# The nine scatters of the output: with and without a wait for the one before

## The chip, the core and the metric

The kernel runs on one core of a Trainium2 chip. The core has five engines, each with a list of instructions of its own: TensorE (PE, matmuls; PEld is its weight load), VectorE (DVE), ScalarE (ACT), GpSimd (POOL) and SyncE (SP). They wait for each other by semaphores. Transfers between the chip's memory and the core's own memory run on 16 DMA engines; they are issued by SyncE (queue q1) and, where an index decides which rows are written or read, by GpSimd (queue q0). The metric is the time of one execution in microseconds of device time, the median of several.

## The reference

Three parts follow each other: causal attention in a window of 128 positions with a linear bias (batch 2, 8 heads, 576 positions, 64 columns), a mixture of 8 experts in which each token goes to the expert with the largest logit, and a second mixture in which each token goes to every expert. There are N = 1152 tokens of D = 512 columns, and the hidden width F is 1024. The last part ends in the output that this change is about:

```python
for e in range(E):
    h = np.maximum(x @ w1[e], 0.0)
    ye = h @ w2[e]
    out += P[:, e:e + 1] * ye
return out.astype(np.float32)
```

`P` are weights of tokens and experts, normalized eight times over experts and over tokens.

## The kernel before, in words

After the first mixture the tokens lie sorted by expert, not in the order of the input. The table `tok_i` (128 rows by 9) holds for each place of the sorted order the token that stands there; it is a permutation of the 1152 tokens, together with the places of its nine columns. It is made on the chip with scatters of line 1021 and read back once. The first mixture takes its tokens with indexed gathers (`load_x`, line 243). Both go through GpSimd's queue and are over early.

The second mixture works on the sorted tokens. Its sums are held in nine tiles `acc[0]` to `acc[8]` of 128 tokens by 512 columns. Expert 0 is done first. The other seven experts are done in 14 passes (`passes`, two for each expert, each with half of the hidden units). In a pass, `group` makes hidden units for a part of the tokens (its matmuls are line 1360, its other work lines 1351 to 1373 on ScalarE and VectorE), and `layer2` multiplies them with the second weights. For each tile `layer2` runs 12 matmuls (line 1391) into one bank of PSUM, and VectorE then adds the bank, weighted by `Pm`, to `acc[s]` (line 1393). Matrix products are made in three parts from values that are split in a high and a low part; GpSimd makes some of the low parts (lines 1247 and 1254).

In the last pass alone, each `acc[s]` is final after line 1393 and goes out at once: GpSimd issues a scatter (line 1395) that writes the 128 rows of the tile to the rows of `out` that `tok_i[:, s]` names. That is 256 KB a scatter, nine in all. The nine sums of the last pass stand one right behind the other on VectorE, in the order of the tiles of two groups (four tiles and then five), and the nine scatters are the last work on GpSimd.

The order on each engine is the order in which the code is written (`in_order` ties each instruction to the one before it on its engine). The waits between engines are put in by the tile framework, by what each instruction reads and writes. It takes a scatter with an index as a write to all of `out`, so that a scatter has to wait for the landing of the scatter before it. A transfer that GpSimd issues takes one of eight semaphore lanes in turn, and it waits until the earlier transfer on its own lane has landed. When the last instruction is done, the engines wait for all lanes and meet in a closing barrier; those instructions have line 1448.

Of the kernel before, what the change touches and what calls it, by code (L numbers as in the profile page):

```python
# [89 lines left out]
def fused_kernel(ctx, tc, q, k, v, wg1, w1, w2, wg2, u1, u2, out, capacity):  # L90
    nc = tc.nc
# [1165 lines left out]
    def run(steps, count=99):  # L1257
        for _ in range(count):
            if next(steps, 0) == 0:
                break  # L1260
# [81 lines left out]
    def bank():  # L1342
        return ring.tile([P, DM], F32, tag="pr", name="pr")
# [39 lines left out]
    def layer2(n, g, steps):  # L1383
        e, r = passes[n]
        for s in TILES[g]:
            run(steps, 2)
            ops = bank()
            m = 0
            for k in range(2 * QP):
                for a, b in ((hT[0], w2p[0]), (hT[0], w2p[1]), (hT[1], w2p[0])):  # L1390
                    nc.tensor.matmul(ops, a[:, k, s * P:(s + 1) * P], b[:, k, :], start=(m == 0), stop=(m == 6 * QP - 1))  # L1391
                    m += 1
            nc.vector.scalar_tensor_tensor(out=acc[s], in0=ops, scalar=Pm[:, s, e:e + 1], in1=acc[s], op0=ALU.mult, op1=ALU.add)  # L1393
            if n == len(passes) - 1:
                nc.gpsimd.indirect_dma_start(  # L1395
                    out=out[:, :], out_offset=IndirectOffsetOnAxis(ap=tok_i[:, s:s + 1], axis=0),
                    in_=acc[s], in_offset=None)
        run(steps)

    last_of.update({k: None for k in last_of})  # L1400
    n0 = len(nc.cur_bb.bb.instructions)
    load_2(0)
    for n in range(len(passes) + 1):
        more = n < len(passes)
        if n == 0:
            run(parts_y(0))
            load_1(1)
        if more:
            for q in range(QP):
                group(q, 0)  # L1410
        if n:
            layer2(n - 1, 1, iter(()))
        if more:
            psteps = parts_2(n)
            weight_sums(n + 1)
            for q in range(QP):
                run(psteps, QP)
                group(q, 1)
            load_2(n + 1)

            def both():
                for st_ in (parts_x(n + 1), parts_y(n + 1)):
                    for _ in st_:
                        yield 1
                load_1(n + 2)

            layer2(n, 0, both() if n + 1 < len(passes) else iter(()))
        in_order(n0)
        n0 = len(nc.cur_bb.bb.instructions)
# [22 lines left out]
```

## Time and profile before

| what | value |
|---|---|
| median of 3 runs | 1060.69 us |
| lowest and highest of the runs | 1059.94 and 1061.14 us |
| time of the profiled execution | 1050.62 us |
| its span, from the first to the last instruction | 1048.4 us |
| mean granted TensorE clock | 0.994 |
| TensorE busy | 1019.7 us, 97% |
| GpSimd busy | 320.1 us, 31% |

The span is what the views of the profile divide. The time of the profiled execution is 2.2 us more than its span, and the median of the runs is 10.07 us above the profiled execution. Times in the views are microseconds from the start of the span. A queue's own instructions, like waits for semaphores, carry a q behind the engine's name and count as no busy time.

### The profile page before, as it was taken

The page shows a single profiled execution, that of the slowest core. Times are in us where ns is not written, and L with a number is a line of the kernel's source. Part 1 is how long each engine was busy: PE and PEld are TensorE (multiplying, and loading weights), DVE is VectorE, ACT ScalarE, POOL GpSimd, SP SyncE. Part 2 cuts the span into 40 slices and gives each one's busy share as a digit, 9 for nine tenths or more (in the row PEclk, how much of TensorE's full clock was granted, in tenths as well). Part 3 has the DMA queues.
Part 4 walks back from the last instruction along what each step waited for, and adds up shares of the span by engine and source line. Part 5 has one row for each costly group of instructions (what it writes and reads, how often), then busy time and mean ns, then how long its engine had stood idle before and what let it go on. Part 6 is the DMA issues. An engine that isn't in the chain of part 4 may idle for free. (4 is left out here: it accounts for less than half of the span.)

```text
span 1048.4 us, 16893 instructions
## 1 busy us (share of the span) xinstructions
PE 1019.7 (97%) x6420; PEld 929.7 (89%) x6420; DVE 674.8 (64%) x1636; ACT 387.1 (37%) x838; POOL 320.1 (31%) x305
## 2 busy tenths in 40 slices
PE   8999999999999999999999999999999999999994
PEld 6888999998889998989899999989899999989893
DVE  7987778777784347575765757574665757575551
ACT  7643577777321313232232323232232323233220
POOL 7433244431200123341323224231333324132122
PEclk9999999999999999999999999999999999999998
DMA  9921599885200102021111202021111202021001
GB/s 244 217 54 52 168 252 228 239 249 197 79 1 1 63 19 81 1 81 41 41 41 41 81 1 81 1 81 42 41 41 41 81 1 81 9 72 41 1 21 70
DMA packets 74104, 83.24 MB, mean 79 GB/s; under 512 B 31585, under 2 KB 45921, under 8 KB 74018
## 3 DMA queue, kind: packets, MB, share of 16 engines
q1 hardware_dynamic: 71906, 76.59, 25.3%
q0 software_dynamic: 2112, 5.52, 1.7%
q8 instruction: 52, 0.85, 0.3%
q14 instruction: 34, 0.28, 0.1%
HBM read 77.37 MB, written 4.73 MB: 78 GB/s over the span
## 5 line engine op out<-in xcount | busy, mean ns | idle before, releaser
L1391 PE MATMUL pr<-w_whi,hT 128*128 128x512 f32 x1008 | 315.8, 390 | 0.3 <-DVE hT L1352 0.3
L1391 PEld LDWEIGHTS pr<-w_whi,hT 128*128 128x128 f32 x1008 | 189.3, 188 | 39.4 <-DVE hT L1352 0.5
L1391 PE MATMUL pr<-w_wlo,hT 128*128 128x512 f32 x504 | 196.5, 390 | 0.0
L1254 POOL TENSOR_TENSOR w_wlo<-r,w_whi 128x512 fp32r<-128x512 f32 x56 | 71.3, 1294 | 291.0 <-ACT w_whi L1253 181.1
L1393 DVE SCALAR_TENSOR_TENSOR acc<-pr,Pm,acc 128x512 f32<-128x512 f32 x126 | 91.2, 744 | 89.8 <-PE pr L1391 89.7
L1351 ACT ACTIVATE hT<-pr 128x256 fp32r<-128x256 f32 (+1 forms) x168 | 69.0, 411 | 175.6 <-DVE pr L1368 175.6
L1352 DVE SCALAR_TENSOR_TENSOR hT<-pr,hT 128x256 fp32r<-128x256 f32 (+1 forms) x168 | 77.0, 458 | 80.1 <-ACT hT L1351 80.1
L1360 PE MATMUL pr<-y_hi,wy 128*128 128x320 f32 (+1 forms) x560 | 122.7, 297 | 0.0
L1391 PEld LDWEIGHTS pr<-w_wlo,hT 128*128 128x128 f32 x504 | 94.7, 188 | 19.5 <-POOL w_wlo L1254 0.5
L1360 PEld LDWEIGHTS pr<-y_hi,wy 128*128 128x128 f32 x560 | 93.8, 188 | 0.3 <-DVE hT L1352 0.3
L1247 POOL TENSOR_TENSOR wy<-r,wy 128x512 fp32r<-128x512 f32 x28 | 40.0, 1428 | 174.2 <-ACT wy L1246 174.2
L191 DVE TENSOR_TENSOR wlo<-w,whi 128x1024 fp32r<-128x1024 f32 x66 | 81.7, 1241 | 3.1 <-issue 3.1
L1360 PE MATMUL pr<-y_lo,wy 128*128 128x256 f32 (+1 forms) x280 | 83.3, 297 | 0.0
L179 ACT CAST whi<-w 128x1024 fp32r<-128x1024 f32 x66 | 69.1, 1050 | 22.4 <-DMA w<-in_moe_w_dram 18.0
L748 PE MATMUL pb<-xt,whi 128*128 128x384 f32 x256 | 74.3, 362 | 2.5 <-issue 1.9
L748 PE MATMUL pb<-h,whi 128*128 128x384 f32 x256 | 75.5, 362 | 1.2 <-DVE t L768 1.2
L1253 ACT CAST w_whi<-r 128x512 fp32r<-128x512 f32 x56 | 33.1, 619 | 94.9 <-PE pr L1391 94.0
L1351 ACT ACTIVATE hT<-h 128x256 fp32r<-128x256 f32 (+1 forms) x56 | 24.9, 445 | 115.4 <-DVE h L1368 115.4
L1360 PE MATMUL pr<-y_hi,wx_wlo 128*128 128x256 f32 (+1 forms) x224 | 64.6, 289 | 0.0
L1360 PE MATMUL pr<-y_hi,wx_whi 128*128 128x256 f32 (+1 forms) x224 | 64.4, 288 | 0.0
L1360 PE MATMUL pr<-y_lo,wx_whi 128*128 128x256 f32 (+1 forms) x224 | 64.4, 288 | 0.0
L1231 POOL TENSOR_TENSOR sums<-r 128x512 f32<-128x512 f32 x28 | 37.1, 1327 | 80.3 <-DMA r<-in_moe_w_dram 45.9
(358 smaller groups left out, 2255.7 us busy)
## 6 DMA issues: line engine op xcount, KB each, us to landing
w<-in_moe_w_dram SPq DMA_DIRECT2D x36, 1024.0 KB, 7.9
r<-in_moe_w_dram SPq DMA_DIRECT2D x56, 512.0 KB, 3.9
kb<-in_k_dram SPq DMA_DIRECT2D x8, 256.0 KB, 4.4
qb<-in_q_dram SPq DMA_DIRECT2D x8, 256.0 KB, 4.5
vb<-in_v_dram SPq DMA_DIRECT2D x8, 256.0 KB, 5.4
xg_d<-xg SPq DMA_DIRECT2D x8, 256.0 KB, 2.6
kb<-in_k_dram SPq DMA_DIRECT2D x2, 128.0 KB, 4.6
qb<-in_q_dram SPq DMA_DIRECT2D x2, 128.0 KB, 4.9
```

The costliest lines, as they stand in the source:

```text
L179: nc.scalar.copy(his[i][:, sl, :], raws[i][:, sl, :])
L191: nc.vector.tensor_tensor(out=los[i][:, sl, :], in0=raws[i][:, sl, :], in1=his[i][:, sl, :].bitcast(F32), op=ALU.subtract)
L748: nc.tensor.matmul(ps[:, 0:2 * W], whi, x.rearrange("p r w -> p (r w)"), start=(m == 0), stop=(m == K - 1))
L1231: nc.gpsimd.tensor_tensor(out=o[:, dst], in0=x, in1=y, op=op_)
L1247: nc.gpsimd.tensor_tensor(out=wy[1][:, i], in0=x, in1=wy[0][:, i].bitcast(F32), op=ALU.subtract)
L1253: nc.scalar.copy(w2p[0][:, k], x)
L1254: nc.gpsimd.tensor_tensor(out=w2p[1][:, k], in0=x, in1=w2p[0][:, k].bitcast(F32), op=ALU.subtract)
L1351: nc.scalar.activation(hi, src, AF.Relu)
L1352: nc.vector.scalar_tensor_tensor(out=lo, in0=src, scalar=0.0, in1=hi.bitcast(F32), op0=ALU.max, op1=ALU.subtract)
L1360: nc.tensor.matmul(ps, a[:, i, c, f], b, start=(c == 0 and m == 0), stop=(c == 1 and m == 2))
L1391: nc.tensor.matmul(ops, a[:, k, s * P:(s + 1) * P], b[:, k, :], start=(m == 0), stop=(m == 6 * QP - 1))
L1393: nc.vector.scalar_tensor_tensor(out=acc[s], in0=ops, scalar=Pm[:, s, e:e + 1], in1=acc[s], op0=ALU.mult, op1=ALU.add)
```

## The change

Each scatter is remembered in a list, and each new one is declared to have no dependency on those remembered, so that the framework puts in no wait between them. The matrix `tok_i` names each row of `out` once, so no two of the scatters write the same row.

```diff
             if n == len(passes) - 1:
-                nc.gpsimd.indirect_dma_start(
+                st_op = nc.gpsimd.indirect_dma_start(
                     out=out[:, :], out_offset=IndirectOffsetOnAxis(ap=tok_i[:, s:s + 1], axis=0),
                     in_=acc[s], in_offset=None)
+
+                for before in stores:
+                    tc.declare_no_dep(st_op.ins, before, reason="rows of different tokens")
+                stores.append(st_op.ins)
         run(steps)
 
+    stores = []
     last_of.update({k: None for k in last_of})
```

The end of GpSimd's list in the kernel before, with what each instruction waits for (`DMASW0` to `DMASW7` are the eight lanes, `DVE` is VectorE, here the sum in `acc`):

```order
L1395 DMA out_dram<-acc,tok_i 1152x512 [waits DMASW3_49,DMASW2_49,DVE_49]
L1395 DMA out_dram<-acc,tok_i 1152x512 [waits DMASW4_49,DMASW3_49,DVE_49]
L1395 DMA out_dram<-acc,tok_i 1152x512 [waits DMASW5_49,DMASW4_49,DVE_49]
L1395 DMA out_dram<-acc,tok_i 1152x512 [waits DMASW6_49,DMASW5_49,DVE_49]
L1395 DMA out_dram<-acc,tok_i 1152x512 [waits DMASW7_49,DMASW6_49,DVE_49]
L1395 DMA out_dram<-acc,tok_i 1152x512 [waits DMASW7_49,DMASW0_49,DVE_49]
L1395 DMA out_dram<-acc,tok_i 1152x512 [waits DMASW1_49,DMASW0_49,DVE_49]
L1395 DMA out_dram<-acc,tok_i 1152x512 [waits DMASW2_49,DMASW1_49,DVE_49]
L1395 DMA out_dram<-acc,tok_i 1152x512 [waits DMASW2_49,DVE_49]
```

From the second on, each has the lane of the scatter before it among its waits; the first takes lane 3, the ninth lane 3 again. The same place in the changed kernel, on the same engine:

```order
L1395 DMA out_dram<-acc,tok_i 1152x512 [waits DMASW3_49,DMASW2_49,DVE_49]
L1395 DMA out_dram<-acc,tok_i 1152x512 [waits DMASW4_49,DVE_49]
L1395 DMA out_dram<-acc,tok_i 1152x512 [waits DMASW5_49,DVE_49]
L1395 DMA out_dram<-acc,tok_i 1152x512 [waits DMASW6_49,DVE_49]
L1395 DMA out_dram<-acc,tok_i 1152x512 [waits DMASW7_49,DVE_49]
L1395 DMA out_dram<-acc,tok_i 1152x512 [waits DMASW0_49,DVE_49]
L1395 DMA out_dram<-acc,tok_i 1152x512 [waits DMASW1_49,DVE_49]
L1395 DMA out_dram<-acc,tok_i 1152x512 [waits DMASW2_49,DVE_49]
L1395 DMA out_dram<-acc,tok_i 1152x512 [waits DMASW3_49,DVE_49]
```

Each has kept the wait for its own lane and for VectorE. The order of the instructions on the five engines is otherwise the same in both kernels; only line numbers behind the change are others (the closing line 1448 is 1453).

## Rows read from the trace of the kernel before

**Rows 1.** Head of the page: span, busy time of each engine
```profile
span 1048.4 us, 16893 instructions
PE 1019.7 (97%) x6420; PEld 929.7 (89%) x6420; DVE 674.8 (64%) x1636; ACT 387.1 (37%) x838; POOL 320.1 (31%) x305
```

**Rows 2.** Table by stretch: length, busy times, granted clock, DMA share, GB/s
```profile
108.00:130.00 22.00, 21.75 (x158) 21.55 (x159) 16.71 (x46) 12.99 (x21) 4.70 (x4) 1.00 0.57 181
155.00:182.00 27.00, 26.02 (x186) 25.62 (x185) 21.44 (x30) 19.96 (x33) 12.60 (x11) 1.00 0.94 248
1009.00:1033.00 24.00, 24.00 (x107) 19.73 (x106) 9.41 (x16) 1.50 (x4) 5.12 (x6) 1.00 0.14 55
1033.00:1048.40 15.40, 0.28 (x2) 0.00 (x0) 0.75 (x1) 0.00 (x0) 3.74 (x4) 0.68 0.17 68
```

**Rows 3.** Chain that ended last, its end: start, length, what
```profile
1037.33 2.54 issue
1039.87 2.71 DMA out_dram<-acc,tok_i
1042.58 0.02 issue
1042.60 0.02 POOLq L1395
...
1043.12 1.18 POOLq L1448
```

**Rows 4.** GpSimd in order of time: start, length, instruction, idle before, releaser
```profile
1015.28 1.20 POOL L1395 DMA_INDIRECT out_dram<-acc,tok_i  x1 [6.54 <-DVE acc L1393]
1019.00 0.96 POOL L1395 DMA_INDIRECT out_dram<-acc,tok_i  x1 [2.52 <-issue]
...
1025.92 0.96 POOL L1395 DMA_INDIRECT out_dram<-acc,tok_i  x1 [2.50 <-DVE acc L1393]
...
1032.91 0.96 POOL L1395 DMA_INDIRECT out_dram<-acc,tok_i  x1 [2.56 <-DMA out_dram<-acc,tok_i]
...
1043.35 0.96 POOL L1395 DMA_INDIRECT out_dram<-acc,tok_i  x1 [2.52 <-DMA out_dram<-acc,tok_i]
```

**Rows 5.** Line 1395, the scatters: ns shortest/median/longest; landing
```profile
L1395 POOL DMA_INDIRECT out_dram<-acc,tok_i x9: 958/958/1202, 1015.3 to 1043.3; - x9
...
DMA to landing us min/median/max: 2.7/2.7/2.9
```

**Rows 6.** VectorE in order of time: the first, third and ninth sum
```profile
1014.23 0.74 DVE L1393 SCALAR_TENSOR_TENSOR acc<-pr,Pm,acc 128x512 f32<-128x512 f32 x1
...
1017.00 0.75 DVE L1393 SCALAR_TENSOR_TENSOR acc<-pr,Pm,acc 128x512 f32<-128x512 f32 x1 [1.37 <-PE pr L1391]
...
1033.32 0.75 DVE L1393 SCALAR_TENSOR_TENSOR acc<-pr,Pm,acc 128x512 f32<-128x512 f32 x1 [1.97 <-PE pr L1391]
```

**Rows 7.** Lines 243 and 1021, indexed gathers and scatters earlier on
```profile
L243 POOL DMA_INDIRECT xw<-xg_d,slot_i x14: 916/1510/1939, 110.5 to 220.5; - x14
...
DMA to landing us min/median/max: 4.9/8.6/12.0
...
L1021 POOL DMA_INDIRECT tok_d<-tid_c,d_i x10: 950/1000/1899, 134.1 to 217.1; - x10
```

**Rows 8.** GpSimd from 110 to 113: two gathers, and their landings
```profile
110.52 0.94 POOL L243 DMA_INDIRECT xw<-xg_d,slot_i  x1 [11.54 <-DVE slot_i L654]
111.76 0.92 POOL L243 DMA_INDIRECT xw<-xg_d,slot_i  x1 [0.31 <-issue]
...
DMA to landing us min/median/max: 4.9/5.3/5.7
```

**Rows 9.** Line 1448 from 1034 on: the closing instructions of the queues
```profile
L1448 SPq EVENT_SEMAPHORE  x13: 17/28/20895, 1025.2 to 1048.4; - x13
...
L1448 POOLq DRAIN  x3: 52/115/4454, 1043.1 to 1048.1; - x3
```

**Rows 10.** DMA queues from 1036 to 1040, one scatter: packets, MB, share
```profile
DMA packets 80, 0.26 MB, mean 66 GB/s; under 512 B 16, under 2 KB 16, under 8 KB 80
...
q0 software_dynamic: 80, 0.26, 16.8%
```

## The prediction

> **What bounds the kernel now.** I read the top of the page first. TensorE is busy for 97% of the span [rows 1], so in nearly all of the 1048.4 us only work on TensorE could be saved. The table by stretch shows that this ends before the kernel does: up to 1033 TensorE is busy all the time at a granted clock of 1.00, and in the 15.4 us after 1033 it has 0.28 us of work, VectorE 0.75 us, ScalarE none [rows 2]. What fills these 15.4 us is the question, and the chain of waits answers it: a scatter of the output, a stretch of "issue", the next scatter, its landing 2.71 us after its start, a semaphore, and the closing instructions of line 1448 [rows 3]. Nothing else stands in that chain.
>
> Next I read GpSimd in order of time. The nine scatters of line 1395 start at 1015.28, 1019.00, and so on to 1043.35 [rows 4]. From the second to the ninth that is (1043.35 - 1019.00)/7 = 3.48 us each. Of it 0.96 us is GpSimd's own work and some 2.5 us idle time. The reader is to see that the idle time has the same length whatever the row names as its cause (issue, VectorE, or the scatter before). Its real cause is in the order with its waits: each scatter from the second on waits for the semaphore lane of the one before it, thus for its landing. A landing comes 2.7 us after the start [rows 5], and 3.48 - 2.71 = 0.77 us later the next one starts.
>
> VectorE, which makes the rows that are scattered, goes faster than that. Its nine sums of line 1393 come in steps of 2.72 us ((1033.32 - 1017.00)/6), the pace of 12 matmuls for a tile [rows 6]. So the scatters fall behind by 3.48 - 2.72 = 0.76 us with each tile, on top of the second one's delay. The last sum ends at 1033.32 + 0.75 = 1034.07, and its scatter starts at 1043.35, 9.28 us later. What is bound by the wait is thus the tail alone: a chain of nine transfers that ends last, beside a TensorE that has been done for ten microseconds.
>
> **The change, part by part.** It adds no instruction to any engine and moves none: TensorE, VectorE, ScalarE and SyncE keep their order, and the nine scatters keep theirs. Up to 1015 us nothing differs, and I count that part as 0.
>
> What it removes is the wait of the second to the ninth scatter for the lane of the one before. Two waits of each scatter stay: for VectorE's sum, and for the earlier use of its own lane. There are eight lanes. For the first eight scatters the lane was last used by the transfers of lines 243 and 1021, all issued by 220.5 us [rows 7]. The ninth has the lane of the first, which lands at 1015.28 + 2.9 = 1018.2 [rows 4, 5], 16 us before the ninth sum is there. So the lanes hold nothing up.
>
> What is late next is VectorE's sum. From the end of a sum to the start of a scatter that waits for nothing else there is one row: the first sum ends at 1014.23 + 0.74 = 1014.97 and its scatter starts at 1015.28, so 0.31 us [rows 4, 6]. GpSimd must also be free. Two indirect transfers with no wait between them start as soon as 0.30 us after the end of GpSimd's part of the one before: 110.52 + 0.94 to 111.76 [rows 8]. Scatter 2 then starts at about 1015.28 + 1.20 + 0.30 = 1016.8 and is out of GpSimd at 1017.7. Scatter 3 waits for its sum, which ends at 1017.75. From there on GpSimd needs 0.96 + 0.30 = 1.26 us in each 2.72 us, so it is never late again. Even the longest GpSimd part of any indirect transfer before, 1.94 us [rows 7], would give 2.24 us, still under 2.72.
>
> The ninth scatter: sum done 1034.07, plus 0.31, starts at 1034.38 in place of 1043.35. The saving is 1043.35 - 1034.38 = 8.97 us.
>
> What follows its start stays: 1048.4 - 1043.35 = 5.1 us to the end of the span. In it are 2.71 us to the landing (SyncE's long wait from 1025.2 of 20.9 us ends there, at 1046.1) and GpSimd's closing drain, 1043.1 + 4.45 = 1047.6 [rows 9], and then a barrier. Whether that drain hangs on the landing or on GpSimd's own end, it moves with the last scatter; TensorE's and VectorE's ends at 1034 are earlier than anything in it. So no part of the 5.1 us is saved.
>
> Does the landing stay at 2.71 us? Data of a scatter moves for some 0.7 us (16.8% of a 4 us stretch for its 80 packets [rows 10]). A scatter every 2.72 us and a landing after 2.71 us means that, but for the first two, hardly any two are in flight together, and no other traffic is left in that stretch: its DMA share of 0.14 before 1033 and 0.17 after is the scatters' own [rows 2]. I take 2.71.
>
> Bounds of what the trace does not show. The start after the sum: 0.31 us from the one row, or 0.77 us, what a scatter takes after a landing now; I take 0.31, since the ninth scatter, like the first, has had time to be decoded. GpSimd's part of the ninth: 0.96 us as in eight of nine [rows 5], or 1.94 as the longest [rows 7], which would put the landing 0.98 later; I take 0.96, as nothing runs beside it. The landing: 2.71, or 4.9 as the quickest of the gathers [rows 7], which is 2.2 more; I take 2.71, being the same transfer at the same load. Below these the saving can hardly go up: the scatter cannot start before 1034.07, which would add 0.31 us. Together the ends are a saving of 9.28 and one of 8.97 - 0.46 - 0.98 - 2.2 = 5.3 us.
>
> The sum: the profiled execution took 1050.62 us with a span of 1048.4; minus 8.97 gives a span of 1039.4 and 1041.65 us. The timed runs have a median of 1060.69, 10.07 us more than the profiled one. The trace has no row for that difference, so I keep it as it is: 1060.69 - 8.97 = 1051.7 us, 0.85% less.
>
> **The rivals.**
> 1. The queue takes one scatter at a time anyway. Then the scatters follow each other by 2.71 us in place of 3.48: the ninth lands at 1015.28 + 9 x 2.71 = 1039.67, against 1043.35 + 2.71 = 1046.06 now. The saving is 6.4 us, 1054.3 us. For it: all scatters go through one queue, q0 [rows 10]. Against it: two gathers of that queue that started 1.24 us apart landed 4.9 and 5.7 us after their starts, so at most 2.1 us apart [rows 8], and only 0.7 us of each scatter is data.
> The Trainium skill has a rule of this kind ("DMA: Bandwidth & Descriptors", section "Rules for kernel authors"): two transfers from one engine do not run side by side but serialize, since both use the same ring on each of the 16 DMA engines. By the whole transfer, that is this rival's 1054.3 us; by the data alone it is 0.7 us in each 2.72, which changes nothing, and the pair of gathers agrees with the second reading.
> 2. Slower: scatters that are let go together get in each other's way. Its place is q0 from 1015.28 on, its price the time per scatter, 4.9 us as with the quickest of the pairs of gathers in place of 3.48, nine in a row: 1015.28 + 9 x 4.9 = 1059.4, 13.3 us later than now, 1074.0 us. It decides from (1046.06 - 1015.28)/9 = 3.42 us per scatter. For it: every gather that had another behind it landed after 4.9 to 12.0 us [rows 7], none after 2.7. Against it: SyncE was loading weights in those stretches, at a DMA share of 0.57 and 0.94, against 0.17 here [rows 2].
> 3. Hidden anyway: in the timed runs the last stage is slower than in the profiled one, and the sums come every 3.48 us or more. Then the wait costs nothing there and the time stays at 1060.7. This needs 0.76 x 8 = 6 of the 10.07 us difference to lie in the last 20 us. For it: nobody sees where the 10.07 us are. Against it: TensorE has no gap and its full clock in that stage [rows 2].
> 4. The change does not do what it says, another wait being in the place of the one removed: also 1060.7. The order speaks against it, by the lanes worked out above.
>
> **How the numbers follow.** The forecast has 0.87, its own range being 1051.1 (the 0.31 less and 0.3 of scatter between runs: the three runs lie 1.2 us apart) to 1053.5 (both of the first two upper bounds and 0.3). Rival 1 has 0.06, rival 2 has 0.03, rivals 3 and 4 together 0.04. The range of 1050.4 to 1054.3 holds the forecast with the spread of two medians, and reaches to rival 1. A measurement of this kernel can tell about 0.2%, 2.1 us, from no change. Faster by more than that: the forecast and rival 1, 0.93. Within it: rivals 3 and 4, 0.04. Slower: rival 2, 0.03.
>
> **What would show it.** In the profile of the changed kernel GpSimd's scatters from the third on should start some 0.3 us after each sum, 2.72 us apart, with idle time before them put down to VectorE; the second at about 1016.8; the last at 1034.4 if the first is at 1015.28; landings of 2.7 us; and some 5 us from the last scatter's start to the end. The span should be near 1039.4. Steps of 2.71 us with no tie to the sums would be rival 1, landings of 4 us and more rival 2. The prediction is wrong if the last scatter starts more than 1.5 us after the last sum, or if the closing part grows over 5.1 us.

## The result and the profile after

The changed kernel took 1050.79 us in the median of 4 runs (1046.78 to 1053.38), the kernel before 1060.91 us (4 runs, 1059.94 to 1065.45). The ratio is 0.9903, with a 95% interval of 0.9877 to 0.9929. The forecast was 1051.7 us; the measured time lies in the prediction's range of 1050.4 to 1054.3 and 0.3 us under the forecast's own range, which began at 1051.1.

The page of the changed kernel, its head and the chain that ended last by line (the line of the closing instructions is 1453 now):

```profile
span 1047.2 us, 16893 instructions
PE 1028.1 (98%) x6420; PEld 936.7 (89%) x6420; DVE 673.8 (64%) x1636; ACT 387.0 (37%) x838; POOL 319.4 (30%) x305
...
PE pr L1391 31%; PE pr L1360 29%; PE ops L1317 5%; PE hps L1277 4%; PE pb L748 1%; POOL out_dram L1395 1%; PE pb L752 1%; DVE wlo L191 0%; DVE tsums L1163 0%; POOL w_wlo L1254 0%; PE lps L1050 0%; POOLq L1453 0%; PE cps L1087 0%; DVE lsb L1054 0%; PE ltp L1057 0%
```

The chain that ended last now goes back through TensorE's matmuls. Before, it consisted of scatters, issue and the closing instructions alone, as far as the view follows it back, to 1036.4 us [rows 3]. But the span is only 1.2 us shorter than before [rows 1], and TensorE was busy for 8.4 us more with as many instructions. To see what the change did, the last stage has to be read by itself. GpSimd and VectorE in order of time, in the changed kernel (in brackets the idle time before and what ended it; "issue" means that the profile shows nothing that was waited for):

```profile
1022.01 0.74 DVE L1393 SCALAR_TENSOR_TENSOR acc<-pr,Pm,acc 128x512 f32<-128x512 f32 x1
...
1023.06 1.20 POOL L1395 DMA_INDIRECT out_dram<-acc,tok_i  x1 [6.54 <-DVE acc L1393]
1024.56 0.96 POOL L1395 DMA_INDIRECT out_dram<-acc,tok_i  x1 [0.30 <-issue]
1025.83 0.96 POOL L1395 DMA_INDIRECT out_dram<-acc,tok_i  x1 [0.30 <-DVE acc L1393]
1028.53 0.96 POOL L1395 DMA_INDIRECT out_dram<-acc,tok_i  x1 [1.74 <-DVE acc L1393]
...
1041.10 0.75 DVE L1393 SCALAR_TENSOR_TENSOR acc<-pr,Pm,acc 128x512 f32<-128x512 f32 x1 [1.97 <-PE pr L1391]
...
1042.13 0.96 POOL L1395 DMA_INDIRECT out_dram<-acc,tok_i  x1 [1.76 <-DVE acc L1393]
```

They answer to [rows 4] and [rows 6]. The last scatter starts 0.28 us after the end of the last sum (1041.85), where it was 9.28 us before. From the third on the scatters come at the pace of the sums. From the end of the last sum to the end of the span it is 1047.21 - 1041.85 = 5.4 us; before it was 1048.43 - 1034.07 = 14.4 us. I call this stretch the tail in what follows. It became 9.0 us shorter.

The scatters' line and the closing line, in answer to [rows 5] and [rows 9]:

```profile
L1395 POOLq EVENT_SEMAPHORE  x9: 17/17/43, 1014.5 to 1039.2; - x9
L1395 POOL DMA_INDIRECT out_dram<-acc,tok_i x9: 955/960/1202, 1023.1 to 1042.1; - x9
...
DMA to landing us min/median/max: 2.7/2.7/2.9
...
L1453 SPq EVENT_SEMAPHORE  x14: 17/28/16293, 1027.3 to 1047.2; - x14
...
L1453 POOLq DRAIN  x3: 52/115/4462, 1041.9 to 1046.9; - x3
```

Landing, GpSimd's own part and the closing drain are what they were. The queue's waits, 2947 ns in the median before, have shrunk to 17 ns: what they wait for is long past. Their line before:

```profile
L1395 POOLq EVENT_SEMAPHORE  x9: 17/2947/3236, 1006.7 to 1042.6; - x9
```

The first sum, though, starts at 1022.01 against 1014.23 [rows 6], 7.8 us later, after instructions that are the same. The table by stretch shows one place where this comes from; the first fence is of the changed kernel, with its last stage below, and the second of the one before (columns as in [rows 2]):

```profile
98.70:112.40 13.70, 13.70 (x66) 11.62 (x67) 6.17 (x42) 1.08 (x5) 1.04 (x1) 0.50 0.05 20
...
1017.00:1041.00 24.00, 24.00 (x106) 19.54 (x105) 9.41 (x16) 1.31 (x3) 7.92 (x8) 1.00 0.20 79
1041.00:1047.20 6.20, 0.06 (x1) 0.00 (x0) 0.75 (x1) 0.00 (x0) 0.96 (x1) 0.76 0.20 79
```

```profile
98.70:112.40 13.70, 13.45 (x111) 12.10 (x110) 9.63 (x50) 4.12 (x9) 1.85 (x3) 1.00 0.27 86
```

For these 13.7 us the granted clock was 0.50, the lower of its two levels, in the profiled execution of the changed kernel, and 1.00 before; TensorE was busy throughout and got through 66 matmuls in place of 111. Both executions are single ones, and the place lies 900 us ahead of the change. So of two profiled executions, the one before was lucky by nearly 8 us, which hides most of the gain in the spans. The tail is free of this: TensorE has no work in it (its last 0.06 us lie ahead of the end of the last sum), and six of the seven traces in which the last scatter starts 0.28 us after its sum, at mean granted clocks of 0.987 to 0.999, have a tail of 5.4 us. The seventh, of the second experiment below, has 5.7, by a closing part that is 0.3 us longer. That is why the experiments are read by the tail.

### The profile page after: what moved, and what is told of

The parts are those of the page before. It is cut to its first block, busy times and chain, and to the rows that moved or that the text cites. A ratio compares the mean times of both kernels' runs of the same rounds, so it can differ in the third digit from the quotient of the medians.

```text
span 1047.2 us, 16893 instructions
## 1 busy us (share of the span) xinstructions
PE 1028.1 (98%) x6420; PEld 936.7 (89%) x6420; DVE 673.8 (64%) x1636; ACT 387.0 (37%) x838; POOL 319.4 (30%) x305
## 4 chain that ended last, share of the span: by engine, by line
PE 71%; issue 2%; DVE 1%; POOL 1%; POOLq 0%; ACT 0%; ACTq 0%
PE pr L1391 31%; PE pr L1360 29%; PE ops L1317 5%; PE hps L1277 4%; PE pb L748 1%; POOL out_dram L1395 1%; PE pb L752 1%; DVE wlo L191 0%; DVE tsums L1163 0%; POOL w_wlo L1254 0%; PE lps L1050 0%; POOLq L1453 0%; PE cps L1087 0%; DVE lsb L1054 0%; PE ltp L1057 0%
## 5 line engine op out<-in xcount | busy, mean ns | idle before, releaser
L179 ACT CAST whi<-w 128x1024 fp32r<-128x1024 f32 x66 | 69.1, 1050 | 19.9 <-DMA w<-in_moe_w_dram 15.4
```

The lines of the kernel that those rows point to most:

```text
L179: nc.scalar.copy(his[i][:, sl, :], raws[i][:, sl, :])
```

## The experiments

**The same kernel, more runs.** No edit.

> The changed kernel once more, against the one before. Theory (the tail alone got shorter, by what the last scatter starts earlier after the last sum): from the end of the last sum to the end of the span 5.4 us, against 14.4 us before, in whatever run; the time about 9.0 us or 0.85% under before, a ratio of 0.9915. Rival (the wait is hidden in timed runs, and the first comparison moved by TensorE's granted clock alone): the same 5.4 us, but a ratio of 0.998 to 1.002 over more rounds.

VectorE's last sum in this run, whose span is 1046.5 us:

```profile
1040.42 0.75 DVE L1393 SCALAR_TENSOR_TENSOR acc<-pr,Pm,acc 128x512 f32<-128x512 f32 x1 [1.97 <-PE pr L1391]
```

Measured: 1047.07 us in the median of 6 runs (1042.11 to 1051.81) against 1059.03 of 17 (1047.91 to 1063.40), ratio 0.9892 with an interval of 0.9845 to 0.9939; tail 5.4 us (1046.54 - 1041.17). The forecast of 0.9915 lies in the interval, no change does not. The spread is wide for a reason: the 17 executions of the kernel before had mean granted clocks of 0.981 to 0.994 and, along with these, spans of 1061.2 to 1045.7 us. The rival is out. But the medians are 12.0 us apart, 3 more than the tails. The six executions of the changed kernel had mean granted clocks of 0.987 to 0.997, in the median 0.9915 against 0.986. By an estimate from the shares of the last stretches (0.68 over 15.4 us before, 0.76 over 6.2 us after) some 0.003 of this is the shorter end itself; the rest, some 0.002 of the span or 2 us, is a kinder clock and not the change.

**The other chain of scatters freed too.** In the changed kernel, the ten scatters of the token table as well:

```diff
-                    nc.gpsimd.indirect_dma_start(
+                    tok_op = nc.gpsimd.indirect_dma_start(
                         out=tok_d[:, :], ...
+                    for before in toks:
+                        tc.declare_no_dep(tok_op.ins, before, ...)
+                    toks.append(tok_op.ins)
```

> The changed kernel with the same declaration also for the ten scatters of the token table (line 1021), five of which sat idle for 29.0 us in all behind each other. Theory (a wait is worth what the chain that ends last holds of it): GpSimd's idle time before these scatters falls from 4 to 7 us each to about 0.3, but between 110 and 220 us TensorE is busy for 96 to 99% and does not wait for them, so the time stays within 0.2% of the changed kernel. Rival (a freed scatter is worth its idle time wherever it stands): several us faster than the changed kernel, up to 29.

The scatters' line in this kernel:

```profile
L1022 POOL DMA_INDIRECT tok_d<-tid_c,d_i x10: 950/1002/1867, 139.6 to 220.6; - x10
its engine sat idle before it (us, times) until:
  issue: 2.3, 10
```

In the changed kernel's own trace the same scatters waited for each other:

```profile
  DMA tok_d<-tid_c,d_i: 27.5, 5
```

GpSimd's idle time before them went from 27.5 us in these five waits to 2.3 us in all, as expected. The time did not follow: 1051.39 us in the median of 12 runs (1043.90 to 1059.05), 0.9938 of the kernel before (0.9904 to 0.9971), against 0.9892 for the changed kernel in the same session. So 25 us of idle time were worth nothing there. The second part of the expectation, "within 0.2% of the changed kernel", did not hold: the medians are 0.4% apart to the bad side. The two intervals overlap, but clock and span of every execution are on record, and at the same mean granted clock the twelve executions are some 2.8 us longer than the six of the changed kernel in that session (by straight lines of span against clock with one common slope; 95% interval 1.1 to 4.6). So it probably loses a little. In the trace it loses in the first mixture: about 600 matmuls take 89.9 us against 85.5 in the changed kernel, at a granted clock of 1.00 in both (the first row is of this kernel, columns as in [rows 2]):

```profile
162.40:252.30 89.90, 86.24 (x602) 84.06 (x601) 68.63 (x92) 62.18 (x107) 31.85 (x31) 1.00 0.85 225
```

```profile
165.10:250.60 85.50, 84.92 (x603) 84.12 (x601) 68.60 (x92) 62.56 (x106) 32.30 (x32) 1.00 0.86 242
```

Traces of kernels that kept this chain of waits lie between 85.3 and 90.0 us in the same stretch, so that the freed scatters are the cause is not shown.

**All scatters held to the end, first try.** The scatters are issued after the last sum, with the last tile's first:

```diff
-            if n == len(passes) - 1:
+            if n == len(passes) - 1 and g == 1 and s == TILES[1][-1]:
+                for t in [s] + TILES[0] + TILES[1][:-1]:
                     st_op = nc.gpsimd.indirect_dma_start(...)   # of acc[t]
                     ...                                         # the declaration, as in the change
```

> All nine scatters are held back until the last sum is done (that tile's scatter stands first, the others behind it), without waits for each other. From the end of the last sum to the end of the span. Theory (GpSimd's part, 0.96 and 0.30 us between, is all that spaces free scatters): the scatters start 1.26 us apart, the last one 0.3 + 1.5 + 7 x 1.26 = 10.6 us after the sum, 15.7 us in all. Rival, the queue takes one at a time: 2.71 us apart, 27 us in all. Rival, scatters in flight together slow each other to 4.9 us: 47 us in all.

```profile
1020.01 1.20 POOL L1396 DMA_INDIRECT out_dram<-acc,tok_i  x1 [6.54 <-DVE acc L1393]
1021.51 0.96 POOL L1396 DMA_INDIRECT out_dram<-acc,tok_i  x1 [0.30 <-issue]
...
1038.05 0.75 DVE L1393 SCALAR_TENSOR_TENSOR acc<-pr,Pm,acc 128x512 f32<-128x512 f32 x1 [1.97 <-PE pr L1391]
...
1039.08 0.95 POOL L1396 DMA_INDIRECT out_dram<-acc,tok_i  x1 [1.77 <-DVE acc L1393]
```

A miss: nothing was held. The first scatter starts long before the last sum, and the tail is 5.4 us as in the changed kernel. The next experiment has the same order in the code without the declaration, and there they are held. So the declaration took away more than the wait: the scatters no longer kept the order in which the code has them, and were placed in the order of their sums.

**The same with the waits.** As above, without the three lines of the declaration.

> As the held run, but each scatter waits for the one before it, as in the kernel before. Theory: 3.48 us apart (0.96 of GpSimd, landing at 2.71, 0.77 until the next start), 0.3 + 8 x 3.48 + 5.1 = 33.2 us from the last sum to the end. Rival, the step of 3.48 us was the pace of the sums in part: nearer to 27 us, or to the 15.7 of the free ones.

VectorE's last sum, which ended at 1035.05, and GpSimd's scatters in this kernel:

```profile
1034.30 0.75 DVE L1393 SCALAR_TENSOR_TENSOR acc<-pr,Pm,acc 128x512 f32<-128x512 f32 x1 [1.97 <-PE pr L1391]
...
1035.35 1.20 POOL L1396 DMA_INDIRECT out_dram<-acc,tok_i  x1 [25.63 <-DVE acc L1393]
1038.57 0.96 POOL L1396 DMA_INDIRECT out_dram<-acc,tok_i  x1 [2.01 <-DMA out_dram<-acc,tok_i]
1041.54 0.96 POOL L1396 DMA_INDIRECT out_dram<-acc,tok_i  x1 [2.01 <-DMA out_dram<-acc,tok_i]
...
1050.98 0.96 POOL L1396 DMA_INDIRECT out_dram<-acc,tok_i  x1 [2.52 <-DMA out_dram<-acc,tok_i]
1053.94 0.96 POOL L1396 DMA_INDIRECT out_dram<-acc,tok_i  x1 [2.00 <-DMA out_dram<-acc,tok_i]
...
1059.92 0.96 POOL L1396 DMA_INDIRECT out_dram<-acc,tok_i  x1 [2.02 <-DMA out_dram<-acc,tok_i]
```

The tail is 1065.0 - 1035.05 = 30.0 us, 3.2 under the theory's 33.2 and 3 over the rival's 27. The chain is there, but its step is not 3.48 us: six of the eight steps are 2.96 to 3.00 us, the first is 3.22 (the first scatter's own part and its landing are 0.24 us longer), and one is 3.48 (to the scatter at 1050.98). The landing takes 2.7 us in all but the first, so from a landing to the next start, which I call the restart, it is 0.27 us here and 0.77 in that one. The waits in the trace show a difference: that scatter has the lane of the one before in a wait instruction of its own ahead of it, and starts 0.73 us after the end of this instruction; the others have it on the scatter itself, which then stands ready to go. In the kernel before, the scatter itself holds the wait for VectorE's sum, and the lane of the one before stands in the instruction ahead. All eight restarts were of the slow kind there, 0.76 to 0.79 us. The place of the wait was not changed by itself in any run.

**Held by data.** VectorE copies the index table behind the last sum, and all scatters read the copy; they do not wait for each other. Against the first try:

```diff
+                nc.vector.tensor_copy(tok_j, tok_i)
                 for t in [s] + TILES[0] + TILES[1][:-1]:
-                    ... IndirectOffsetOnAxis(ap=tok_i[:, t:t + 1], axis=0),
+                    ... IndirectOffsetOnAxis(ap=tok_j[:, t:t + 1], axis=0),
```

> The changed kernel, with all nine scatters held by data: their index table is copied by VectorE behind the last sum, and the scatters read the copy, without waits for each other. From the end of the last sum to the end of the span. Theory (GpSimd's part is all that spaces free scatters, and the queue takes several at a time): the copy some 0.2 us, the first scatter 0.3 us behind it, then 1.5 and 7 x 1.26 us to the last one's start and 5.1 us to the end, 15.9 us in all, with landings of 2.7 to 2.9 us. Rival, the queue takes one at a time: 2.71 us apart, 27 us in all. Rival, scatters in flight together slow each other to 4.9 us: landings of 4 us and more, 20 to 47 us in all.

VectorE and GpSimd in order of time:

```profile
1046.86 0.75 DVE L1393 SCALAR_TENSOR_TENSOR acc<-pr,Pm,acc 128x512 f32<-128x512 f32 x1 [1.97 <-PE pr L1391]
1047.53 0.16 DVE L1395 COPY tok_j<-tok_i 128x9 int32<-128x9 int32 x1
...
1047.99 1.20 POOL L1397 DMA_INDIRECT out_dram<-acc,tok_j  x1 [25.71 <-DVE tok_j L1395]
1049.50 0.96 POOL L1397 DMA_INDIRECT out_dram<-acc,tok_j  x1 [0.30 <-issue]
1050.77 0.96 POOL L1397 DMA_INDIRECT out_dram<-acc,tok_j  x1 [0.31 <-issue]
...
1058.35 0.96 POOL L1397 DMA_INDIRECT out_dram<-acc,tok_j  x1 [0.30 <-issue]
```

The landings, and the DMA engines' busy tenths in 40 slices of 0.325 us from 1049 to 1062:

```profile
DMA to landing us min/median/max: 2.7/2.7/2.9
...
DMA  0079308930891099019902980397049505950000
```

The tail is 1063.4 - 1047.61 = 15.8 us, as the theory had it. Nine scatters run 1.26 us apart, two or three in flight at any time, and each lands in the same 2.7 us as when alone. The nine blocks of data in the DMA row stand apart with gaps between. So at this pace the queue neither takes one at a time nor slows them. The same nine scatters, held behind the last sum with the waits, needed 30.0 us.

**One wait put back.** The ninth scatter alone waits for the eighth:

```diff
-                for before in stores:
+                for before in stores if len(stores) < 8 else stores[:-1]:
```

> The changed kernel, but the ninth scatter alone waits for the eighth. From the end of the last sum to the end of the span, 5.4 us in the changed kernel. Theory (a wait costs by how much landing and restart, 2.71 + 0.77, are longer than the step of the sums, 2.72): the ninth starts 0.76 us later, 6.1 us in all. Rival (each wait costs the 2.5 us that GpSimd sat idle): 7.9 us.

```profile
1041.37 0.96 POOL L1395 DMA_INDIRECT out_dram<-acc,tok_i  x1 [1.76 <-DVE acc L1393]
...
1043.06 0.75 DVE L1393 SCALAR_TENSOR_TENSOR acc<-pr,Pm,acc 128x512 f32<-128x512 f32 x1 [1.97 <-PE pr L1391]
...
1044.84 0.96 POOL L1395 DMA_INDIRECT out_dram<-acc,tok_i  x1 [2.51 <-issue]
```

The tail is 1049.9 - 1043.81 = 6.1 us, as expected. GpSimd sits idle 2.51 us before the ninth scatter, but the scatter comes only 0.75 us later after its sum (1.03 us in place of 0.28). One wait costs 0.75 us, not the idle time beside it.

**Waits for the one two before.**

```diff
-                for before in stores:
+                for before in stores[:-2] + stores[-1:]:
```

> The changed kernel, but each scatter waits for the one two before it, so that two may be in flight. Theory (two steps of the sums, 5.44 us, cover landing and restart, 3.48 us): as the changed kernel, 5.4 us from the last sum to the end. Rival (the wait itself, its instruction and the restart of the queue after it, costs some 0.5 to 0.8 us even where the landing is long past): 5.9 to 6.2 us.

```profile
1028.85 0.97 POOL L1395 DMA_INDIRECT out_dram<-acc,tok_i  x1 [0.30 <-issue]
1031.05 0.96 POOL L1395 DMA_INDIRECT out_dram<-acc,tok_i  x1 [1.23 <-issue]
1032.81 0.96 POOL L1395 DMA_INDIRECT out_dram<-acc,tok_i  x1 [0.81 <-DVE acc L1393]
...
1045.39 0.75 DVE L1393 SCALAR_TENSOR_TENSOR acc<-pr,Pm,acc 128x512 f32<-128x512 f32 x1 [1.97 <-PE pr L1391]
...
1046.41 0.96 POOL L1395 DMA_INDIRECT out_dram<-acc,tok_i  x1 [1.76 <-DVE acc L1393]
```

The tail is 1051.5 - 1046.14 = 5.4 us. Only the third scatter is held up, since the first two come close behind each other; by the fourth this is made up. A wait whose landing is past costs nothing here (the last scatter starts 0.28 us after its sum), and at this pace of the sums two in flight are as good as no waits.

**The sums slowed, with and without waits.** In the last pass the 12 matmuls of a tile run twice; once with the scatters of the kernel before and once with those of the changed one:

```diff
+            for again in range(2 if n == len(passes) - 1 else 1):
                 m = 0
                 for k in range(2 * QP):
                     ...
```

> The kernel before, with the 12 matmuls of each tile of the last pass run twice (the second time over the first), so that the sums come 5.44 us apart in place of 2.72. Theory (the wait decides only where the sums come faster than every 3.48 us): each scatter starts 0.3 us after its sum, 5.4 us from the last sum to the end, as without waits. Rival (the chain of nine waits costs its 8 x 0.76 us or more at any pace): 12 to 14.4 us.

> The changed kernel with the same doubled matmuls in the last pass. Theory: 5.4 us from the last sum to the end, the same as with the waits, so that the change is worth nothing at this pace. Rival: 6 us or more less than with the waits.

With waits, VectorE's last sum and GpSimd's last two scatters:

```profile
1063.95 0.96 POOL L1396 DMA_INDIRECT out_dram<-acc,tok_i  x1 [4.48 <-DVE acc L1394]
...
1068.36 0.75 DVE L1394 SCALAR_TENSOR_TENSOR acc<-pr,Pm,acc 128x512 f32<-128x512 f32 x1 [4.69 <-PE pr L1392]
...
1069.39 0.96 POOL L1396 DMA_INDIRECT out_dram<-acc,tok_i  x1 [4.47 <-DVE acc L1394]
```

Without:

```profile
1059.88 0.75 DVE L1394 SCALAR_TENSOR_TENSOR acc<-pr,Pm,acc 128x512 f32<-128x512 f32 x1 [4.69 <-PE pr L1392]
...
1060.91 0.96 POOL L1396 DMA_INDIRECT out_dram<-acc,tok_i  x1 [4.48 <-DVE acc L1394]
```

Both tails are 5.4 us (1074.5 - 1069.11 and 1066.0 - 1060.63), and both last scatters start 0.28 us after their sum. At this pace the waits cost nothing. The spans differ by 8.5 us all the same; the mean granted clocks are 0.989 and 0.999, and the whole difference is there before the first scatter, which starts at 1025.90 with waits and at 1017.42 without. Whoever compared the two spans would have found the saving of the change in a place where it has none.

## Why the prediction was right, and where it was off

The saving was put at 8.97 us; the tails differ by 9.0 us. Its steps one by one:

- That the wait binds the tail alone, by the sums' 2.72 us being shorter than a scatter's 3.48: shown from both sides. At sums of 5.44 us the same waits cost nothing, and one wait put back costs 0.75 us. The prediction says that the nine sums come in steps of 2.72 us; this holds from the third on. The first three lie closer, 2.77 us for two steps [rows 6]. Six steps that are 0.76 us too long make 4.6 of the 9.0 us, and these first ones the rest: the scatters took 1043.35 - 1015.28 = 28.07 us from the first to the ninth, the sums 1033.32 - 1014.23 = 19.09 [rows 4, 6], which is 8.98 less. The prediction's sum has both, since it goes by the ninth scatter's start.
- The start 0.31 us after the sum: 0.28 to 0.31 us. The second scatter 1.50 us after the first: as forecast. From the third on at the pace of the sums: so it was.
- Lanes hold nothing up: the ninth scatter has the first one's lane and starts 0.28 us after its sum like the rest. (The read-back of `tok_i` is one more earlier user of the lanes that the prediction leaves out; it was issued at 222.5 us, as long past.)
- Landing 2.71 and some 5.1 us from the last scatter's start to the end: 5.1 us in the changed kernel.
- Rivals 1 and 2, one at a time or slower together: both out by the run held by data, 1.26 us apart with landings of 2.7 to 2.9 us. The rule of the Trainium skill that the prediction sets beside rival 1 ("DMA: Bandwidth & Descriptors", section "Rules for kernel authors"), which stands there for transfers to disjoint partition halves, holds here, if at all, only for the data on the DMA engines, some 0.7 us of each scatter.
- Rival 3, hidden anyway: the mechanism is real, as the slowed sums show, but the sums of the kernel itself kept 2.72 us, from the third on, in every trace that left its matmuls as they were, and the medians of the timed runs fell by 10 and 12 us.
- Rival 4, another wait in the place of the one removed: out, the queue's waits fell from 2947 ns in the median to 17.

Two steps were off without hurting the number. The restart of 0.77 us after a landing was taken for one figure, as an upper bound: it is 0.27 us where the wait stands on the scatter itself. And the spread of the executions was put at 0.3 us, from three runs that lay 1.2 us apart, and the least difference that can be told at 0.2%. The intervals came out as 0.26% to either side with four runs each and as 0.47% in the second session. Behind this is the step "the trace has no row for that difference, so I keep it as it is". The 10.07 us between the profiled execution and the median are most likely, for the greater part, time at a granted clock of 0.50, which the traces show, while TensorE works, in the first 300 us alone: in the 17 executions of the kernel before, 0.001 of the mean granted clock goes with about 1 us of span, and the profiled execution had 0.994, the median 0.986. For the first four timed executions of the kernel before no clock is on record.

That the median came out within 1 us of the forecast is therefore in part luck. The same two kernels were 12.0 us apart in the second session, and the changed kernel's 1047.07 us there lies below the whole range of the prediction; the kernel before was quicker there, too, at 1059.03. What confirms the mechanism is the tail.

## What to carry to other kernels

A chain of transfers with waits costs what it takes longer, from its first start to its last, than the work that feeds it (28.07 against 19.09 us here), and only if it ends last: compare these two, step by step, not the idle time of the engine that waits. Twenty-five microseconds of such idle time taken away in the middle of this kernel were worth nothing, and nine taken away at its end were worth all of it. Where a change works on one stage, read that stage from an event ahead of it (here the last sum) to the end, since spans of two single executions may differ by as much for other reasons.

## What the runs showed that I had not expected

- The granted clock falls to 0.50 for stretches of 3.4 to some 17 us in the first 300 us, in places and lengths that differ from execution to execution: of the changed kernel's two traces, one has its longest such stretch at 98.7 us for 13.7 us, the other at 96.7 for 17.1. In the slowed pair, one kernel had a mean clock of 0.989 and one 0.999, and 8.5 us lay between them. Three runs within 1.2 us of each other were no measure of this: 17 executions of the kernel before lay between 1047.91 and 1063.40 us.
- Where a wait stands is worth half a microsecond: the restart after a landing was 0.27 us in the seven cases with the wait on the scatter, 0.76 to 0.79 us with it in an instruction ahead.
- The declaration also took away the order of the scatters among each other. In the changed kernel this does no harm; where all of them are meant to come after an event, data can hold them there, as the copy of the index table did.
